# Retention feeding an erf-gated two-layer network: keys and queries of the first chunks loaded ahead of values and handled one by one, first pieces of the second layer's weights converted in single blocks

## The chip, the cores and the metric

The kernel runs on one core of a Trainium2 chip. The metric is the device time of one execution in microseconds (us). Before the change the median of seven runs is 683.71 us, with the lowest at 683.50 and the highest at 684.05 us. The core has one queue of instructions per engine, worked off in order: PE (TensorE, matrix products), DVE (VectorE, elementwise), ACT (ScalarE, copies and functions), POOL (GpSimd) and SP (SyncE, which here only issues transfers). ACT can issue transfers too, on a queue of its own. A trace of one execution shows, for every engine, when each instruction started, how long it took and what its engine had waited for.

## The reference

Two blocks follow each other. The first is a retention over 4 sequences of 768 steps, 8 heads of 64 numbers; the second is a two-layer network on the 3072 resulting rows of 512 numbers:

```python
for t in range(S):
    state = gamma[None, :, None, None] * state + np.einsum('bhd,bhe->bhde', k[:, :, t], v[:, :, t])
    y[:, :, t] = scale * np.einsum('bhd,bhde->bhe', q[:, :, t], state)
...
h = x @ w_in                                   # 512 -> 2048
sp = np.maximum(h, 0.0) + np.log1p(np.exp(-np.abs(h)))
g = h * erf(sp)
return (g @ w_out).astype(np.float32)          # 2048 -> 512
```

Keys, queries and values are 32-bit floats. The two weight matrices arrive as 64-bit floats, and the kernel turns them into 32-bit floats itself.

## The kernel before, in words

**Retention.** A sequence is cut into chunks of 128 steps, 24 chunks in all, numbered j. `load(j)` issues the transfers of a chunk's keys, queries and values, 256 KB each. `ret_scale(j)`, called `K_`, multiplies keys and queries by powers of the decay on DVE (L403, one instruction of 1024 columns for both). `ret_transpose(j)`, called `T`, transposes the keys and then the queries on PE, four instructions each (L418), and ACT copies each result out of PSUM (L424). `ret_scores(j)`, `S_`, forms the products of keys and queries on PE (L431) in two PSUM banks. `ret_mask(j)`, `M`, multiplies both banks by the causal mask on DVE (L443, two instructions of 512 columns). `ret_out(j)`, `O_`, adds on PE the part that comes from the state (L471), the part that comes from this chunk's values (L478) and the chunk's own contribution to the state (L487); ACT copies the output out (L498). `ret_add(j)`, `A`, adds the contribution to the state on DVE (L611, L613). `by` is the decay over one chunk; from it and `d_k` come the scales `kq_s` of all chunks, computed by a few small instructions on DVE and POOL (`other_scales` finishes them).

**Network.** The first four chunks make one column block of 512 rows. Its first layer has 16 pieces `hidden(g, u)` (four matrix products each, L664), four per group g; after each, ACT copies the result out (L682). `gate(g)` runs softplus (L624) and erf (L634) on ACT, each after a load of its function table; `gated(g)` multiplies on DVE (L653). `project(g, tt)` is the second layer (L700), 16 products a group into four PSUM tiles. The work on rows after the first 512 uses seven products in place of eight on sums of blocks (L757, L829) and is not touched by the change.

**Weights.** They are converted in 16 pieces in the order in, in, in, in, out, out, in, in, out, out and so on (`conversion(n)`): DVE masks the exponent (L213), ACT turns it into a scale (L214), DVE extracts and combines the mantissa (L217, L222, L225) and multiplies (L231). The first four pieces are converted in two halves of 512 columns; from the fifth on a piece is one block of 1024 columns. From the sixth on, the L213 of the following piece is slipped in ahead of L225, so that ACT's share is ready when its turn comes. `need(...)` runs the conversion up to a named block before its first use; `pace(n)` and `pace_around(n)` run further steps of it between the other work, by a running account `room`.

**What sets the order.** The program is written in the order in which each engine's queue works it off; there is no scheduler. DVE, ACT and PE each stop at the first instruction whose inputs or buffers are not there, and all behind it waits. The pool `ps_r` has two PSUM tiles in use for transposes, scores and outputs after the first four chunks: the outputs of chunk 5 go into the two tiles from which its mask L443 has read the scores. The transfers stand on SP's queue in the order k0, q0, v0, k1, v1, k2, v2, k3, q3, first half of weight piece 0, v3, other weights; q1 and q2 are issued by ACT. `keep_warm(n)` issues n products of the identity on PE whose result nobody uses (L377), each seen as two matmul records: 16 ahead of the first transposes and 3 after them.

Of the kernel before, what the change touches and what calls it, by code (L numbers as in the profile page):

```python
# [12 lines left out]
F32 = mybir.dt.float32  # L13
# [3 lines left out]
ALU = mybir.AluOpType  # L17
PSUM = bass.MemoryType.PSUM

P = 128  # L20
C = 128
TCH = 512
FG = 4
# [22 lines left out]
def kernel(  # L46
# [35 lines left out]
    ctx.enter_context(tc.manual_schedule())  # L82


    KQ, V, KB = {}, {}, {}

    NB = JPC + 2
# [12 lines left out]
    def load(j):  # L100
        b, c = divmod(j, NC)
        if j == JPC - 1:

            x = act.tile([P, N], F32, name="e", bufs=1)
            KQ[j] = x[:, : 2 * d_model].rearrange("p (i h d) -> p i h d", i=2, h=H)
            V[j] = x[:, 2 * d_model : 3 * d_model].rearrange("p (h d) -> p h d", h=H)
        else:
            KQ[j] = loads.tile([P, 2, H, D], F32, name="kq")
            V[j] = loads.tile([P, H, D], F32, name="v")
        now = slice(c * C, (c + 1) * C)  # L110
        if j >= NB:
            KB[j] = loads.tile([P, HP * C], F32, name="kb", bufs=2)
            nc.sync.dma_start(KQ[j][:, 0], k[b, :, now, :].rearrange("h p d -> p h d"))
            load_blocks(KQ[j][:, 1].rearrange("p h d -> p (h d)"), q[b, :, now, :])
            load_blocks(KB[j], k[b, :, now, :])
        for i, src in enumerate((k, q) if j < NB else ()):

            queue = nc.scalar if i and 0 < j < 3 else nc.sync
            queue.dma_start(KQ[j][:, i], src[b, :, now, :].rearrange("h p d -> p h d"))  # L119
        if j == JPC - 1:  # L120
            load_piece(0, 0)
        nc.sync.dma_start(V[j], v[b, :, now, :].rearrange("h p d -> p h d"))  # L122

    kq_s = const.tile([P, NC, 2, H], F32, name="kq_s")
    d_k = const.tile([P, H], F32, name="d_k")
# [61 lines left out]
    def conversion(n):  # L187

        which, i = pieces[n]
        half, s, at = i // 4, i % 4 // 2, i % 2

        for part in range(2) if n < 4 else (None,):
            words = raws[place[n]].bitcast(U32)
            if which == "in":
                f = slice(at * 2 * P, (at + 1) * 2 * P)
                if part is not None:
                    f = slice((at * 2 + part) * P, (at * 2 + part + 1) * P)
                to = w_in_sb[:, s, 2 * half : 2 * half + 2, :, f].rearrange("p d k f -> p (d k) f")  # L200
            else:
                to = w_out_sb[:, s, 2 * half : 2 * half + 2, at * 2 : at * 2 + 2, :].rearrange(
                    "p d f c -> p d (f c)"
                )
            words = words.rearrange("p (a b w) -> p a b w", a=to.shape[1], w=2)
            number, power = (
                x.rearrange("p (a b) -> p a b", a=to.shape[1]) for x in (numbers, powers[n % 2])
            )
            if part is not None:
                f = slice(part * P, (part + 1) * P)  # L210
                words, number, power = words[:, :, f], number[:, :, f], power[:, :, f]
            lo, hi = words[:, :, :, 0], words[:, :, :, 1]
            nc.vector.tensor_scalar(power, hi, 0x7FF00000, None, op0=ALU.bitwise_and)  # L213
            nc.scalar.activation(power, power, AF.Relu, bias=below, scale=8.0)  # L214
            if part is None:
                yield
            nc.vector.tensor_scalar(  # L217
                number, hi, 0xFFFFF, 1 << 20, op0=ALU.bitwise_and, op1=ALU.bitwise_or
            )
            yield  # L220
            numberf = number.bitcast(F32)
            nc.vector.scalar_tensor_tensor(numberf, number, 2.0**32, lo, op0=ALU.mult, op1=ALU.add)  # L222
            if part is None:
                yield
            nc.vector.scalar_tensor_tensor(  # L225
                power, hi, 1 << 31, power, op0=ALU.bitwise_and, op1=ALU.bitwise_or
            )
            if part != 0:
                load_pieces_after(n)
            yield  # L230
            nc.vector.scalar_tensor_tensor(  # L231
                to, numberf, 2.0**-52, power.bitcast(F32), op0=ALU.mult, op1=ALU.mult,
            )
            done.update((which, 2 * i + u) for u in (range(2) if part is None else (part,)))
            yield
# [18 lines left out]
    def weights():  # L254


        pending = [conversion(n) for n in range(n_p)]
        begun = 0
        for n, steps in enumerate(pending):
            for k, _ in enumerate(steps, start=begun):  # L260
                yield
                if n > 4 and n + 1 < n_p and k == 2:
                    next(pending[n + 1])
                    yield
            begun = int(n > 4)
            if pieces[n] == ("out", 5):
                yield from sums("in", 0)

# [25 lines left out]
    ident = const.tile([P, P], F32, name="ident")  # L294
    make_identity(nc, ident)
    nc.scalar.dma_start(d_k, decay_k)
    for s in range(2):
        nc.scalar.dma_start(d_s[:, s], decay_s[s * D : s * D + 1, :].to_broadcast([P, HP]))
    load(0)

    nc.scalar.copy(idle_out, ident[:, :1])
    for j in range(1, JPC):
        load(j)
    load_piece(0, 1)
    for n in range(1, 4):
        load_piece(n, 0, 1)
    load(JPC)

    causal = const.tile([P, C], F32, name="causal")
    nc.gpsimd.memset(causal, 1.0)  # L310
# [20 lines left out]


    by = const.tile([P, H], F32, name="by")
    nc.vector.reciprocal(by.rearrange("p (h s) -> p s h", s=2), d_s)
    for c in range(1, NC):
        nc.gpsimd.tensor_tensor(kq_s[:, c, 0], kq_s[:, c - 1, 0], by, op=ALU.mult)

    def other_scales():
        query_scale(slice(1, NC))

# [24 lines left out]
    QT, KT, SC, AM, XC, SU = {}, {}, {}, {}, {}, {}  # L367

    psum_turn = itertools.cycle((ps_r, ps_h))
    early = True  # L370


    idle = ps_o.tile([P, P], F32, name="o0")
# [2 lines left out]
        for _ in range(n):  # L376
            nc.tensor.matmul(idle, ident, ident, start=True, stop=True)  # L377

    keep_warm(16)

    def ret_psum(pool=None):

# [2 lines left out]

    scaled = set()

    def ret_scale(j):
        if j >= NJ:
            return  # L390
        scaled.add(j)
        if j >= NB:
            nc.vector.tensor_tensor(
                KQ[j][:, 0], KQ[j][:, 0],
                kq_s[:, j % NC, 0, :, None].to_broadcast([P, H, D]), op=ALU.mult,
            )
            for i, x in enumerate((KB[j], KQ[j][:, 1].rearrange("p h d -> p (h d)"))):
                x = x.rearrange("p (u a d) -> p u a d", u=HP, d=32)
                by = kq_b[:, j % NC, i, :, :, None].to_broadcast([P, HP, 4, 32])
                nc.vector.tensor_tensor(x, x, by, op=ALU.mult)  # L400
            return
        by = kq_s[:, j % NC, :, :, None].to_broadcast([P, 2, H, D])
        nc.vector.tensor_tensor(KQ[j], KQ[j], by, op=ALU.mult)  # L403
        pace(-1.1)

    def ret_transpose(j):
        assert j in scaled
        if j >= NB:
            for name, store, x in (
# [3 lines left out]
                nc.vector.transpose(store[j].rearrange("p u t -> p (u t)"), x)  # L413
            return
        for i, (name, store) in enumerate((("k", KT), ("q", QT))):
            p = ret_psum()
            for u in range(HP):
                nc.tensor.transpose(  # L418
                    p[:, u, :],
# [25 lines left out]
            )  # L445
        pace(-1.2)

    RP = {}

    def ret_out(j, between=None, copies=True):  # L450
        c = j % NC
        m, i = divmod(j, JPC)
        if i == 0:
            XC[m] = ret.tile([P, HP, TCH], F32, name="xT")

        if between is None:
            pp = [ret_psum() for _ in range(2)]
        else:
            pp = [ps_o.tile([P, HP, C], F32, name=f"o{r + 1}") for r in range(2)]

        def place(h):
            return pp[h % 2][h // 4 * D : (h // 4 + 1) * D, h % 4 // 2, :]
# [20 lines left out]
        if c < NC - 1:  # L483
            new = SU[j] = pp[0][:, 2:, :].rearrange("p a (b d) -> p (a b) d", d=D)
            for h in range(H):
# [2 lines left out]
                    new[r * D : (r + 1) * D, h // 2, :], KQ[j][:, 0, h, :], V[j][:, h, :],  # L488
                    start=False, stop=True, skip_group_check=True,
                )  # L490
        RP[j] = pp
        if copies:
            ret_copy(j)

    def ret_copy(j):
        m, i = divmod(j, JPC)
        for r in range(2):
            nc.scalar.copy(XC[m][:, r::2, i * C : (i + 1) * C], RP[j][r][:, :2, :])  # L498
        pace(2.5)


# [117 lines left out]
    def gate(g):  # L619
# [3 lines left out]
        E[g] = act.tile([P, N], F32, name=name, bufs=1)  # L623
        nc.scalar.activation(E[g], HS[g], AF.Softplus)  # L624

        if g:
            gate_erf(g)

    def gate_erf(g):
# [59 lines left out]
    def project(g, tt):  # L689
# [3 lines left out]
        if g:  # L693
            of = [(tt, u) for u in range(FG)]
        else:
            of = [(step % 2 * 2 + i // 2, step // 2 * 2 + i % 2) for i in range(4)]
        need("out", g * FG + max(u for _, u in of))
        for tt, u in of:
            ft = g * FG + u
# [174 lines left out]
    )  # L874


    K_(0)
    other_scales()
    T(0)
    keep_warm(3)  # L880
    for j in range(JPC - 2):
        S_(j)

        K_(j + 1)
        if j:
            A(j - 1)
        T(j + 1)
        M(j)
        O_(j)


    S_(JPC - 2)
    A(JPC - 3)
    M(JPC - 2)
    ret_out(JPC - 2, copies=False)
    K_(JPC - 1)

    next(weight_steps)
    T(JPC - 1)
    ret_copy(JPC - 2)  # L900
    need("in", 0)
    S_(JPC - 1)
    A(JPC - 2)
    M(JPC - 1)
    need("in", 1)
    early = False
    ret_out(JPC - 1, lambda: hidden_of(0, slice(TCH - C)))
    room = 0.0


# [24 lines left out]
    for g in range(G0):  # L935
# [10 lines left out]
        if g:  # L946
            for tt in range(TT):
                project(g - 1, tt)
                if g == 1 and tt < 2:
                    waiting.append((K_, 5) if tt else (M, 4))  # L950
                elif g == G0 - 1 and tt == 0:
                    waiting.extend([(K_, JPC + 2), (T, JPC + 2)])
                elif g == G0 - 1 and tt == 1:
# [132 lines left out]
```

## Time and profile before

| what | value |
|---|---|
| median of 7 runs | 683.71 us |
| the profiled execution | 684.01 us, span 682.3 us |
| PE busy | 676.3 us (99% of the span) |
| DVE busy | 389.8 us (57%); 57.35 of the 60 us from 25 to 85 us |
| ACT busy | 256.0 us (38%) |
| bytes moved | 47.65 MB, a mean of 70 GB/s; 192 to 260 GB/s in the first 68 us |

Times in the trace are counted from the start of the span. The profiled execution lies 0.30 us above the median and outside its span 1.7 us pass. Three stages matter here. Up to about 25 us PE works on the retention of the first four chunks, and inputs arrive. From 25 to about 110 us PE has work without gaps, and DVE is nearly full as well, since it converts all weights in that time. After that DVE and ACT have time to spare. "Busy" of PE is modelled, and the share over the whole span says little of the first stage, which is 4% of it.

### The profile page before, as it was taken

The page shows a single profiled execution, that of the slowest core. Times are in us where ns is not written, and L with a number is a line of the kernel's source. Part 1 is how long each engine was busy: PE and PEld are TensorE (multiplying, and loading weights), DVE is VectorE, ACT ScalarE, POOL GpSimd, SP SyncE. Part 2 cuts the span into 40 slices and gives each one's busy share as a digit, 9 for nine tenths or more (in the row PEclk, how much of TensorE's full clock was granted, in tenths as well). Part 3 has the DMA queues.
Part 4 walks back from the last instruction along what each step waited for, and adds up shares of the span by engine and source line. Part 5 has one row for each costly group of instructions (what it writes and reads, how often), then busy time and mean ns, then how long its engine had stood idle before and what let it go on. Part 6 is the DMA issues. An engine that isn't in the chain of part 4 may idle for free.

```text
span 682.3 us, 14444 instructions
## 1 busy us (share of the span) xinstructions
PE 676.3 (99%) x6214; PEld 578.6 (85%) x6214; DVE 389.8 (57%) x609; ACT 256.0 (38%) x291; POOL 5.8 (1%) x21
## 2 busy tenths in 40 slices
PE   9999999999999999999999999999999999999998
PEld 8744544587999999999999999999999999999996
DVE  4899999585945634643553564555544554343224
ACT  3368362424424234144144242341441441423431
POOL 2000000100000000000000000000000000000000
PEclk9999999999999999999999999999999999999999
DMA  9999644333412322222321222222312200000000
GB/s 192 227 260 238 164 125 103 62 61 63 114 35 45 76 37 42 75 41 37 78 45 32 63 46 45 68 42 44 72 35 49 58 18 2 1 32 1 1 32 32
DMA packets 156528, 47.65 MB, mean 70 GB/s; under 512 B 143024, under 2 KB 147376, under 8 KB 156464
## 3 DMA queue, kind: packets, MB, share of 16 engines
q1 hardware_dynamic: 153952, 46.19, 31.2%
q8 instruction: 49, 0.80, 0.5%
q10 hardware_dynamic: 2512, 0.53, 0.5%
q14 instruction: 15, 0.12, 0.1%
HBM read 40.39 MB, written 6.29 MB: 68 GB/s over the span
## 4 chain that ended last, share of the span: by engine, by line
PE 96%; SPq 2%; DMA 1%; DVE 0%; ACT 0%; issue 0%; DVEq 0%
PE hp L757 37%; PE o L829 36%; PE hp L664 8%; PE o L700 8%; PE r L543 1%; PE hp L508 1%; SPq L119 1%; PE o L579 1%; DMA w_out_sb<-in_moe_w_in_dram 1%; PE r L431 1%; PE hp L558 1%; SPq L122 1%; PE r L558 1%; PE r L478 0%; PE r L418 0%; PE r L579 0%
## 5 line engine op out<-in xcount | busy, mean ns | idle before, releaser
L757 PE MATMUL hp<-xs,w_in_sb 128*128 128x128 f32 x1280 | 149.7, 275 | 0.0
L757 PEld LDWEIGHTS hp<-xs,w_in_sb 128*128 128x128 f32 x1280 | 147.8, 192 | 1.6 <-issue 0.5
L829 PE MATMUL o<-w_out_sb,h 128*128 128x256 f32 x640 | 141.7, 379 | 0.0
L829 PEld LDWEIGHTS o<-w_out_sb,h 128*128 128x128 f32 x640 | 121.6, 190 | 16.5
L757 PE MATMUL hp<-xT,w_in_sb 128*128 128x128 f32 x960 | 113.7, 275 | 0.0
L757 PEld LDWEIGHTS hp<-xT,w_in_sb 128*128 128x128 f32 x960 | 111.9, 192 | 1.9 <-issue 1.0
L829 PE MATMUL o<-w_out_sb,e 128*128 128x256 f32 x480 | 112.1, 383 | 0.0
L653 DVE TENSOR_TENSOR e<-h,e 128x1024 f32<-128x1024 f32 x42 | 49.5, 1221 | 100.0 <-ACT e L634 100.0
L829 PEld LDWEIGHTS o<-w_out_sb,e 128*128 128x128 f32 x480 | 88.2, 190 | 11.6
L664 PE MATMUL hp<-xT,w_in_sb 128*128 128x512 f32 (+2 forms) x144 | 56.8, 548 | 0.0
L782 DVE TENSOR_TENSOR h<-h,hp 128x512 f32<-128x512 f32 x20 | 13.8, 688 | 72.3 <-PE hp L757 72.3
L624 ACT ACT_TABLE_LOAD x24 | 30.8, 1283 | 60.8 <-issue 45.4
L664 PEld LDWEIGHTS hp<-xT,w_in_sb 128*128 128x128 f32 x144 | 25.7, 190 | 26.7 <-issue 24.3
L634 ACT ACTIVATE e<-e 128x2048 f32<-128x2048 f32 (+1 forms) x23 | 42.1, 1836 | 0.2
L624 ACT ACTIVATE e<-h 128x2048 f32<-128x2048 f32 x22 | 42.0, 1910 | 0.2
L770 DVE TENSOR_TENSOR h<-h,hp 128x512 f32<-128x512 f32 x20 | 13.8, 688 | 41.9 <-PE hp L757 41.9
L775 ACT COPY h<-hp 128x512 f32<-128x512 f32 x20 | 11.7, 586 | 61.0 <-PE hp L757 61.0
L780 ACT COPY h<-hp 128x512 f32<-128x512 f32 x20 | 11.7, 585 | 60.3 <-PE hp L757 60.3
L773 ACT COPY h<-hp 128x512 f32<-128x512 f32 x20 | 11.7, 585 | 57.1 <-PE hp L757 57.1
L597 ACT COPY xT<-r 128x256 f32<-128x256 f32 x32 | 10.4, 375 | 54.8 <-PE r L543 54.8
L634 ACT ACT_TABLE_LOAD x24 | 30.8, 1283 | 0.4
L768 ACT COPY h<-hp 128x512 f32<-128x512 f32 x20 | 11.8, 588 | 48.6 <-PE hp L757 48.6
(136 smaller groups left out, 673.9 us busy)
## 6 DMA issues: line engine op xcount, KB each, us to landing
w_out_sb<-in_moe_w_out_dram SPq DMA_DIRECT2D x14, 512.0 KB, 5.7
kq<-in_k_dram SPq DMA_DIRECT2D x23, 256.0 KB, 3.9
v<-in_v_dram SPq DMA_DIRECT2D x23, 256.0 KB, 3.1
out_dram<-r SPq DMA_DIRECT2D x23, 256.0 KB, 3.1
kq<-in_q_dram SPq DMA_DIRECT2D x288, 16.0 KB, 1.8
kb<-in_k_dram SPq DMA_DIRECT2D x288, 16.0 KB, 1.7
w_in_sb<-in_moe_w_in_dram SPq DMA_DIRECT2D x8, 512.0 KB, 6.9
w_out_sb<-in_moe_w_in_dram SPq DMA_DIRECT2D x8, 256.0 KB, 7.4
```

The costliest lines, as they stand in the source:

```text
L558: nc.tensor.matmul(other[a][own, u % 2, D:] if crossed else pp[a][own, u % 2, t], V[j][t, 2 * u + r, :], AM[j][t, r, u, :D], start=crossed ...
L624: nc.scalar.activation(E[g], HS[g], AF.Softplus)
L634: nc.scalar.activation(E[g][:, half], E[g][:, half], AF.Erf)
L653: nc.vector.tensor_tensor(E[g][:, half], HS[g][:, half], E[g][:, half], op=ALU.mult)
L664: nc.tensor.matmul(HP_[ft][:, t], w_in_of(ft, kk), XC[0][:, kk, t], start=(kk == 0), stop=(kk == n_k - 1),)
L700: nc.tensor.matmul(O[0][tt].rearrange("p (d c) -> p d c", d=2), E[g][:, u * TCH + tt * P : u * TCH + (tt + 1) * P], w_out_of(ft), start=(f ...
L757: nc.tensor.matmul(bank[:, u, :], w_in_sb[:, s, IN[a], kk, u * P : (u + 1) * P], XS[m][b][:, kk, :], start=(p in (1, 2, 5) and u == 0 and ...
L768: nc.scalar.copy(h["11"], flat)
L770: nc.vector.tensor_tensor(h["11"], h["11"], flat, op=ALU.add)
L773: nc.scalar.copy(h["12"], flat)
L782: nc.vector.tensor_tensor(h["12"], h["12"], flat, op=ALU.add)
L829: nc.tensor.matmul(O[m][i][:, half, :], G[g][a][:, u * P : (u + 1) * P], w_out_sb[:, s, OUT[b], u, :], start=i not in started, stop=(s == ...
```

## The change

- Transfers of chunks 0 to 3: all on SP, in the order k0, q0, k1, q1, v0, k2, q2, v1, k3, q3, v2, first half of weight piece 0, v3. `d_s` is one transfer of both halves.
- Keys and queries of these chunks are scaled by two instructions of 512 columns and transposed separately; the scores, masks, outputs and state additions stand between them in a new order. The scales of chunk 1 are computed right after the first keys are scaled (`second_scales`). The outputs of chunks 0 to 3 go into the four tiles of `ps_o`.
- Identity products: 7, 2, 1 and 2 at four places.
- `A(2)` stands before the conversion of the first half of weight piece 0 (`need("in", 0)`).
- The fifth and sixth piece of weights (the first two of the second layer) are converted in two halves each, without the early L213 of the next. `project(0, tt)` takes block tt for all four row tiles, in place of two blocks for two tiles.
- erf of group 1 is issued after `project(0, 0)`, behind one more conversion step, and `M(4)`, `K_(5)` after `project(0, 2)`, behind the conversion of the seventh piece.

```diff
         for i, src in enumerate((k, q) if j < NB else ()):
-            queue = nc.scalar if i and 0 < j < 3 else nc.sync
-            queue.dma_start(KQ[j][:, i], src[b, :, now, :].rearrange("h p d -> p h d"))
-        if j == JPC - 1:
-            load_piece(0, 0)
-        nc.sync.dma_start(V[j], v[b, :, now, :].rearrange("h p d -> p h d"))
+            nc.sync.dma_start(KQ[j][:, i], src[b, :, now, :].rearrange("h p d -> p h d"))
+        if not early:
+            load_values(j)
...
-        for part in range(2) if n < 4 else (None,):
+        for part in range(2) if n < 6 else (None,):
...
-                if n > 4 and n + 1 < n_p and k == 2:
+                if n > 5 and n + 1 < n_p and k == 2:
                     next(pending[n + 1])
                     yield
-            begun = int(n > 4)
+            begun = int(n > 5)
...
-    for s in range(2):
-        nc.scalar.dma_start(d_s[:, s], decay_s[s * D : s * D + 1, :].to_broadcast([P, HP]))
+    nc.scalar.dma_start(d_s, decay_s[::D].rearrange("(o s) h -> o s h", o=1).to_broadcast([P, 2, HP]))
     load(0)
     nc.scalar.copy(idle_out, ident[:, :1])
     for j in range(1, JPC):
         load(j)
+        load_values(j - 1)
+    load_piece(0, 0)
+    load_values(JPC - 1)
     load_piece(0, 1)
...
+    def second_scales():
+        nc.vector.reciprocal(by.rearrange("p (h s) -> p s h", s=2), d_s)
+        nc.vector.tensor_tensor(kq_s[:, 1, 0], kq_s[:, 0, 0], by, op=ALU.mult)
+        query_scale(1)
+        for c in range(2, NC):
+            nc.gpsimd.tensor_tensor(kq_s[:, c, 0], kq_s[:, c - 1, 0], by, op=ALU.mult)
...
-    keep_warm(16)
+    keep_warm(7)
...
-        by = kq_s[:, j % NC, :, :, None].to_broadcast([P, 2, H, D])
-        nc.vector.tensor_tensor(KQ[j], KQ[j], by, op=ALU.mult)
+        part = slice(i, i + 1) if i is not None else slice(2)
+        x = KQ[j][:, part]
+        by = kq_s[:, j % NC, part, :, None].to_broadcast([P, x.shape[1], H, D])
+        nc.vector.tensor_tensor(x, x, by, op=ALU.mult)
...
-        if g:
+        if g > 1:
             gate_erf(g)
...
-            of = [(step % 2 * 2 + i // 2, step // 2 * 2 + i % 2) for i in range(4)]
+            of = [(i, step) for i in range(TT)]
...
-    K_(0)
-    other_scales()
-    T(0)
-    keep_warm(3)
-    for j in range(JPC - 2):
-        S_(j)
-        K_(j + 1)
-        if j:
-            A(j - 1)
-        T(j + 1)
-        M(j)
-        O_(j)
-    S_(JPC - 2)
-    A(JPC - 3)
-    M(JPC - 2)
-    ret_out(JPC - 2, copies=False)
-    K_(JPC - 1)
-    next(weight_steps)
-    T(JPC - 1)
-    ret_copy(JPC - 2)
-    need("in", 0)
-    S_(JPC - 1)
-    A(JPC - 2)
-    M(JPC - 1)
+    K_(0, 0)
+    second_scales()
+    T(0, 0)
+    keep_warm(2)
+    K_(0, 1)
+    T(0, 1)
+    keep_warm(1)
+    K_(1, 0)
+    T(1, 0)
+    S_(0)
+    K_(1, 1)
+    T(1, 1)
+    keep_warm(2)
+    other_scales()
+    M(0)
+    S_(1)
+    K_(2, 0)
+    T(2, 0)
+    O_(0)
+    M(1)
+    K_(2, 1)
+    T(2, 1)
+    A(0)
+    O_(1)
+    K_(3, 0)
+    T(3, 0)
+    S_(2)
+    A(1)
+    M(2)
+    O_(2)
+    K_(3, 1)
+    T(3, 1)
+    A(2)
+    need("in", 0)
+    S_(3)
+    M(3)
     need("in", 1)
...
-                if g == 1 and tt < 2:
-                    waiting.append((K_, 5) if tt else (M, 4))
+                if g == 1 and tt == 0:
+                    need("out", 1)
+                    next(weight_steps)
+                    gate_erf(1)
+                elif g == 1 and tt == 2:
+                    need("in", 2 * FG + 1)
+                    waiting.extend([(M, 4), (K_, 5)])
```

## The prediction

> **What bounds the kernel now.** I read the page's chain of work first, then busy time by stretch, then the timelines of the first 95 us, since the change touches nothing later. The chain's shares by engine and two stretches (us, busy time of PE, PEld, DVE, ACT, POOL, clock, DMA share, GB/s):
>
> ```profile
> PE 96%; SPq 2%; DMA 1%; DVE 0%; ACT 0%; issue 0%; DVEq 0%
> ...
> 25.00:45.00 20.00, 20.00 (x109) 11.50 (x106) 18.20 (x34) 9.04 (x14) 0.00 (x0) 1.00 1.13 256
> 45.00:65.00 20.00, 20.00 (x67) 9.55 (x66) 19.39 (x23) 16.09 (x17) 0.00 (x0) 1.00 1.07 247
> 65.00:85.00 20.00, 20.00 (x103) 10.06 (x103) 19.76 (x23) 8.32 (x11) 0.00 (x0) 1.00 0.66 167
> ```
>
> PE has no gap from 25 us on, so a change ahead of that counts only if PE also stays fed. DVE has 2.65 idle us in these 60. The timeline of DVE (start, duration, line, idle before):
>
> ```profile
> 11.04 0.69 DVE L443 TENSOR_TENSOR am<-r,causal 128x512 f32<-128x512 f32 x1 [0.47 <-PE hp L431]
> ...
> 19.46 0.69 DVE L443 TENSOR_TENSOR am<-r,causal 128x512 f32<-128x512 f32 x1 [0.25 <-PE hp L431]
> 20.07 0.68 DVE L443 TENSOR_TENSOR am<-hp,causal 128x512 f32<-128x512 f32 x1
> 20.67 1.22 DVE L403 TENSOR_TENSOR e<-e,kq_s 128x1024 f32<-128x1024 f32 x1
> 21.80 0.42 DVE L213 TENSOR_SCALAR w_out_sb<-w_out_sb 128x512 uint32<-128x512 uint32 x1
> ...
> 24.53 0.41 DVE L611 TENSOR_TENSOR state<-state,r 128x256 f32<-128x256 f32 x1
> 25.18 0.69 DVE L443 TENSOR_TENSOR am<-r,causal 128x512 f32<-128x512 f32 x1 [0.24 <-PE hp L431]
> ...
> 86.83 1.23 DVE L222 SCALAR_TENSOR_TENSOR w_out_sb<-w_out_sb,w_in_sb 128x1024 f32<-128x1024 uint32 x1
> 87.98 1.28 DVE L443 TENSOR_TENSOR am<-r,causal 128x512 f32<-128x512 f32 x2
> ```
>
> The weight conversion starts at 21.80, and behind it stands everything up to M(5) at 87.98. The timeline of PE at both ends, and L471's own waits:
>
> ```profile
> 1.46 6.79 PE L377 MATMUL o<-ident 128*128 128x128 f32 x32 [1.46 <-POOL ident masks.py:199]
> 8.09 0.60 PE L418 MATMUL r<-ident,kq 128*128 128x128 f32 x4
> ...
> 89.24 0.73 PE L471 MATMUL r<-qT,state 64*64 64x128 f32 x16
> 89.91 1.09 PE L478 MATMUL r<-am,v 128*64 128x128 f32 x16
> ...
>   DVE am L443: 0.8, 1
> ```
>
> O(5) may overwrite its two PSUM tiles only when M(5) has read them, the second at 87.98+1.28 = 89.26. PE arrives at 89.24. So at this place DVE and PE finish together: PE gains nothing here unless M(5) comes earlier, and any delay of M(5) reaches the end. ACT in the stretch where the change alters the conversion:
>
> ```profile
> 48.40 0.59 ACT L682 COPY h<-hp 128x512 f32<-128x512 f32 x1 [1.15 <-PE hp L664]
> 49.34 1.15 ACT L214 ACTIVATE w_out_sb<-w_out_sb,below 128x1024 uint32<-128x1024 uint32 x1 [0.35 <-DVE w_out_sb L213]
> 50.51 1.28 ACT L634 ACT_TABLE_LOAD   x1
> 51.80 1.91 ACT L634 ACTIVATE e<-e 128x2048 f32<-128x2048 f32 x1
> 53.62 0.57 ACT L682 COPY h<-hp 128x512 f32<-128x512 f32 x1
> ```
>
> Now ACT forms the fifth piece's scale once, ahead of erf's table load.
>
> **Part 1, transfers and early chunks: where the conversion starts.** I work at the clock of the profiled execution, where a filler pass takes 6.79/32 = 0.21 us and a transpose after 8 us 0.11.
>
> Transfers. Landing is issue plus the listed time: k0 0.81+3.2 = 4.0, q0 1.31+4.4 = 5.7, v0 1.94+4.9 = 6.8, k1 2.92+5.8 = 8.7, q1 4.05+5.2 = 9.3, v1 4.39+6.0 = 10.4. On one queue I give places instead: k1 third at 6.8, q1 fourth at some 8.1, v0 fifth at 9.3, k2 sixth at 10.4 (before 5.38+7.5 = 12.9, for which DVE waited 0.54). SP issues q1 and q2 too (0.4 to 1.4 us each), but it runs 5 us ahead of the landings. The values come up to 3 us later and are used after 12.7; covered. The weights keep their places (13.78+6.2 = 20.0).
>
> Chain. K(0,0) 512 wide 0.69, ends 4.7; its transposes 4 x 0.21 and two fillers end 6.5. The two d_s transfers landed at 4.2 and 5.5, which bounds the single one; I take 5.2. Four small instructions at 0.22, then K(0,1) to 6.75; its transposes end 7.7. Behind a filler, T(1,0) and ACT's copy (0.58), S(0) runs from 8.7 and takes 1.09, so M(0) is at 9.85 against 11.04. K(1,1) and the other scales end 9.35, POOL's four products before that: covered. M(0) and K(2,0) fill DVE to 11.75; S(1) holds PE to 12.2 and T(2,0) to 12.7; O(0) takes 0.82+0.67, ACT's copy 0.38 (A waits for it in the trace), A(0) 0.42: 15.1. O(1) 0.6+0.82+0.67, T(3,0) 0.5 and S(2) 1.09 lead to M(2) at 18.9 against 19.46.
>
> So the chunks gain 0.55. But the conversion had begun 2.34 after M(2) (a second mask and K(3)). Now A(2) stands ahead of it: O(2) ends 2.6 after M(2) (19.46 to 22.08), copy 0.4, A(2) 0.34, with handovers 3.5. It starts at 22.4, **0.6 later**, though its data is there at 20.0. Seven fillers fewer save nothing further, since PE waits at these places.
>
> **Part 2, DVE from the conversion's start to M(5), 66.18 us before.**
> - Out: A(2) 0.33, the wait ahead of M(3) 0.24, 0.3 of two waits of L225 for ACT (0.76, 0.44), 0.16 ahead of `gated(0)`: -1.0.
> - Two pieces in halves: four blocks of 2.74 (26.39 to 29.11 and the like) for two of 4.97 (48.62 to 53.59): +1.0.
> - In the changed order one L222 of 1024 columns stands behind M(5): -1.15.
> - New wait 1. The second half's scale stands on ACT behind erf(0) and a copy. From the first half's L213: ACT starts at 0.45, then 0.63 + 1.29 + 1.82 + 0.47 + 0.72 (the pitches of the rows above, halves from the 512-wide L214) = 5.4. DVE reaches its L225 at 4.15 (2.74 and three steps). It waits **1.25**, and `gated(0)` behind it.
> - New wait 2. The sixth piece's second scale stands behind softplus(1): 0.45 + 0.63 + 1.29 + 1.82 + 0.72 = 4.9 against 4.15: **0.78**.
>
> Moved: M(4) now stands behind the seventh piece. From K(5) to M(5) are 19.7 us (68.28 to 87.98); M(4)'s 1.2 join that stretch, and L222, L213 and L225 (1.14, 0.60, 1.25) and the L222 of 1.15 leave it, so M(4) comes 16.8 before M(5), at 72.6. O(4) takes its tiles at 74.1 by PE's gain of 0.4: covered by 0.2 (second mask 73.9); if M(5) came later, M(4) would too, and PE would lose the same time there first, not twice. erf(1) moves from 64.90 to some 66, used by `gated(1)` after M(4): covered.
>
> Together +0.85. Bounds of the two waits: 0, if ACT gets ahead, and 3.2 each (a table load and a function, 1.28+1.91), if ACT reaches them late; the sums of rows lie between and I keep them.
>
> **Sum.** M(5) moves to 87.98+0.6+0.85 = 89.4, PE's second L471 from 89.31 to 90.75. PE itself would be ready at 88.8: the first layer starts behind the first conversion (22.4+2.8 = 25.2) at 25.25 against 25.68. The other needs are met (`project(0,1)` needs out 1 near 57, PE is there at 60). PE stands still for 1.9 us, and what follows is unchanged: 684.01 + 1.4 = 685.4 for an execution like the profiled one, which lies 0.3 above the median: **685.1 us**.
>
> **A rule beside a row.** The row: 28 filler passes of 0.21 us pass without a gap from 1.46 to 7.6 before the pace doubles. With 7 fillers there are gaps, of 0.15 us near 4.7 and of 0.3 near 6.6. If they don't matter, the above stands. If 6.1 us without a gap are needed, counted from 6.8, the clock opens at 12.9: 5.3 us at half pace cost 2.65, of which waits cover some 0.6, so +2.0 and 687.1.
>
> The Trainium skill, "TensorE: Matmul & The Clock Gate", Part 1, says that the clock opens after a free-running window of 3413 ns has been busy, whatever the number of matmuls; seven fillers last 3.0 us. If a gap spoils a window, its estimate is an opening between 10.2 and 13.6, and 686 to 687.4.
>
> **Rivals.**
> - Late clock, 687.1, as worked out. For it: no gapless 6 us before 6.8. Against: the gaps are a tenth of the time.
> - ACT's waits are hidden (the copies and functions come earlier than DVE): 2.03 goes, M(5) is at 87.4, and PE arrives by its own gain of 0.4: 683.6, less 0.3, **683.3**. Against: both queues are in order, and erf needs all of `h`.
> - The other side, faster: the chunks end so early that the conversion starts as its data lands, at 20.0. That is 1.8 earlier; with +0.85, M(5) gains 1.0: 682.7. It decides when the first L213 starts before 20.95. Against: M(2) would have to start at 16.5.
> - No effect: the waits gone (2.03) and gains lost alike, 683.7.
>
> **How the numbers follow.** About 0.2% (1.4 us: 682.3 and 685.1) is what a measurement can tell. Forecast 0.45, half of it above 685.1; late clock 0.28; ACT's waits hidden 0.15; the early conversion 0.07; no effect 0.05. Slower 0.22+0.28 and a little for larger waits, 0.55; same 0.40; faster 0.05, from the early conversion with ACT's waits hidden as well. Range from 683.3 to 687.2; the forecast's own is 684.4 to 685.8.
>
> **What would show it.** First L213 near 22.4, behind A(2); two idle times of DVE ahead of L230 (the old L225) ended by ACT, 1.25 and 0.78; the fifth M near 89.4 and PE idle some 1.9 ahead of the state part of O(5). The pace of transposes near 8 us (0.11 or 0.21) tells of the clock. I am wrong if the first conversion starts before 21, or if DVE doesn't wait for ACT between 50 and 63 us.

## The result and the profile after

The changed kernel takes 685.34 us (median of 15 runs; 14 of them between 685.14 and 685.61, one at 687.17), against 683.64 us for the kernel before (35 runs). The ratio is 1.0026, with a 95% interval of 1.002 to 1.0033. The change made the kernel 1.7 us slower; the prediction was 685.1 us, 0.24 below the measured median. Its profiled execution took 685.3 us with a span of 683.6.

In the changed kernel the lines have moved: the mask is L460, the state addition L620, the conversion L218 to L236 (ACT's part L219, the instruction that needs it L230), the first layer L673, the state part of an output L486, the second layer L709.

The chain of work of the changed kernel, shares of the span by engine. Before, DVE had 0% of it; now it passes through DVE:

```profile
PE 89%; DVE 6%; ACT 2%; issue 2%; DMA 1%; SPq 0%; ACTq 0%; DVEq 0%
```

Busy time by stretch (us, PE, PEld, DVE, ACT, POOL, clock, DMA share, GB/s). PE was busy all the time from 25 us on (the last stretch of before stands first here, the others stand with the prediction); now it stands still in three of the four stretches:

```profile
85.00:95.00 10.00, 10.00 (x64) 5.19 (x61) 9.83 (x12) 6.86 (x9) 0.00 (x0) 1.00 0.52 171
...
25.00:45.00 20.00, 19.82 (x90) 11.26 (x91) 18.67 (x35) 9.56 (x14) 0.00 (x0) 1.00 1.06 226
45.00:65.00 20.00, 20.00 (x67) 9.65 (x66) 17.35 (x31) 14.19 (x17) 0.00 (x0) 1.00 1.04 244
65.00:85.00 20.00, 19.48 (x97) 9.54 (x97) 19.76 (x22) 9.78 (x13) 0.00 (x0) 1.00 0.71 175
85.00:95.00 10.00, 9.34 (x63) 4.93 (x62) 9.86 (x12) 4.81 (x7) 0.00 (x0) 1.00 0.52 179
```

The first of the three is the wait for the first converted weights at 25 us. DVE lost 2 us between 45 and 65 us (19.39 busy before, 17.35 now). The timeline of DVE tells where (start, duration, line, idle time before and what ended it):

```profile
18.75 0.69 DVE L460 TENSOR_TENSOR am<-r,causal 128x512 f32<-128x512 f32 x1 [0.84 <-PE hp L448]
...
21.89 0.42 DVE L620 TENSOR_TENSOR state<-state,o 128x256 f32<-128x256 f32 x1 [1.25 <-ACT xT L507]
22.23 0.42 DVE L218 TENSOR_SCALAR w_out_sb<-w_out_sb 128x512 uint32<-128x512 uint32 x1
...
53.63 0.69 DVE L230 SCALAR_TENSOR_TENSOR w_out_sb<-w_out_sb 128x512 uint32<-128x512 uint32 x1 [1.31 <-ACT w_out_sb L219]
...
62.15 0.69 DVE L230 SCALAR_TENSOR_TENSOR w_in_sb<-w_out_sb,w_in_sb 128x512 uint32<-128x512 uint32 x1 [0.83 <-ACT w_in_sb L219]
...
80.29 0.41 DVE L620 TENSOR_TENSOR state<-state,r 128x256 f32<-128x256 f32 x1
...
89.33 1.28 DVE L460 TENSOR_TENSOR am<-r,causal 128x512 f32<-128x512 f32 x2
```

The two waits for ACT stand in the second halves of the fifth and the sixth weight piece, as predicted, and M(5), the mask of chunk 5, starts at 89.33. What ACT did ahead of the first of these waits, on its own timeline: the first half's scale, then erf's table load, erf, a copy, and only then the second half's scale, although its input had been there since 51.3.

```profile
48.56 0.72 ACT L219 ACTIVATE w_out_sb<-w_out_sb,below 128x512 uint32<-128x512 uint32 x1
49.30 1.28 ACT L643 ACT_TABLE_LOAD   x1
50.59 1.92 ACT L643 ACTIVATE e<-e 128x2048 f32<-128x2048 f32 x1
52.41 0.56 ACT L691 COPY h<-hp 128x512 f32<-128x512 f32 x1
52.88 0.72 ACT L219 ACTIVATE w_out_sb<-w_out_sb,below 128x512 uint32<-128x512 uint32 x1
```

And what PE then waited for, on its timeline. It stops ahead of the second half of T(5), because A(4) on DVE has not yet read the PSUM tile that these transposes overwrite, and again ahead of O(5), because M(5) has not read its two. The 32 products of the second layer behind O(5) start at 92.28; before (the last line) they started at 90.93:

```profile
25.18 2.82 PE L673 MATMUL hp<-xT,w_in_sb 128*128 128x384 f32 x8 [0.67 <-DVE w_in_sb L236]
...
80.76 0.66 PE L435 MATMUL r<-ident,kq 128*128 128x128 f32 x4 [0.52 <-DVE state L620]
...
90.07 0.43 PE L486 MATMUL r<-qT,state 64*64 64x128 f32 x2 [0.50 <-DVE am L460]
90.67 0.66 PE L486 MATMUL r<-qT,state 64*64 64x128 f32 x14 [0.17 <-DVE am L460]
...
92.28 14.00 PE L709 MATMUL o<-w_out_sb,r 128*128 128x512 f32 x32
...
90.93 14.00 PE L700 MATMUL o<-w_out_sb,r 128*128 128x512 f32 x32
```

The spans of the two profiled executions differ by 1.3 us, the start of these products by 1.35: the whole difference has arisen by then.

### The profile page after: what moved, and what is told of

Same layout as the page of the kernel before. It is cut to its first block, busy times and chain, and to the rows that moved or that the text cites. A ratio compares the mean times of both kernels' runs of the same rounds, so it can differ in the third digit from the quotient of the medians.

```text
span 683.6 us, 14431 instructions
## 1 busy us (share of the span) xinstructions
PE 674.6 (99%) x6200; PEld 575.7 (84%) x6200; DVE 391.4 (57%) x626; ACT 256.9 (38%) x293; POOL 5.9 (1%) x20
## 4 chain that ended last, share of the span: by engine, by line
PE 89%; DVE 6%; ACT 2%; issue 2%; DMA 1%; SPq 0%; ACTq 0%; DVEq 0%
PE hp L766 37%; PE o L838 36%; PE o L709 6%; PE hp L673 3%; PE r L552 1%; PE hp L517 1%; PE o L588 1%; DMA kq<-in_k_dram 1%; DVE w_out_sb L230 1%; DVE w_in_sb L230 1%; DVE w_out_sb L222 1%; PE r L448 1%; PE hp L567 1%; PE o L493 1%; PE r L567 1%
## 5 line engine op out<-in xcount | busy, mean ns | idle before, releaser
L673 PE MATMUL hp<-xT,w_in_sb 128*128 128x512 f32 (+2 forms) x144 | 56.8, 548 | 0.7 <-DVE w_in_sb L236 0.7
L633 ACT ACT_TABLE_LOAD x24 | 30.8, 1283 | 60.8 <-issue 45.4
L673 PEld LDWEIGHTS hp<-xT,w_in_sb 128*128 128x128 f32 x144 | 25.7, 190 | 27.4 <-issue 24.8
L784 ACT COPY h<-hp 128x512 f32<-128x512 f32 x20 | 11.7, 586 | 61.0 <-PE hp L766 61.0
L789 ACT COPY h<-hp 128x512 f32<-128x512 f32 x20 | 11.7, 585 | 60.3 <-PE hp L766 60.3
L782 ACT COPY h<-hp 128x512 f32<-128x512 f32 x20 | 11.7, 585 | 57.1 <-PE hp L766 57.1
L643 ACT ACT_TABLE_LOAD x24 | 30.8, 1283 | 0.4
```

Of the source, the lines that this page charges most:

```text
L643: nc.scalar.activation(E[g][:, half], E[g][:, half], AF.Erf)
L673: nc.tensor.matmul(HP_[ft][:, t], w_in_of(ft, kk), XC[0][:, kk, t], start=(kk == 0), stop=(kk == n_k - 1),)
```

## The experiments

The start of the second layer's products behind O(5), "the mark" from here on, is read in every trace; the part of the span behind it was 591.3 or 591.4 us in all of them. The theory (D) was that time is lost only by way of DVE's queue: what stands ahead of M(5) in that queue, and when it starts. The rivals were that the clock opens later (C), that the new transfers cost or bring something by themselves (T), and that the halves and their waits cost time wherever the masks stand (W).

### Each part alone

The changed kernel with the conversion, erf of group 1, `project(0, tt)`, `M(4)` and `K_(5)` as before:

```diff
-        for part in range(2) if n < 6 else (None,):
+        for part in range(2) if n < 4 else (None,):
...
-        if g > 1:
+        if g:
             gate_erf(g)
...
-                if g == 1 and tt == 0:
-                    need("out", 1)
-                    next(weight_steps)
-                    gate_erf(1)
-                elif g == 1 and tt == 2:
-                    need("in", 2 * FG + 1)
-                    waiting.extend([(M, 4), (K_, 5)])
+                if g == 1 and tt < 2:
+                    waiting.append((K_, 5) if tt else (M, 4))
```

> The changed kernel with the old conversion of the fifth and sixth weight piece (whole blocks), the old place of erf(1), the old order of project(0, tt) and the old places of M(4) and K(5): the chunk part of the change alone. Theory D (DVE's queue up to M(5) sets the end; what made it longer are two waits for ACT of 1.31 and 0.83): the first conversion starts at 22.2 as in the changed kernel, both waits are gone, M(5) stands near 87.5, and PE is held up by less than 0.3 us at O(5): 683.2, 0.4 below the kernel before. Theory C (the later opening of the clock or the gaps in the first 10 us cost the time): 685.3, since that stage is unchanged. Theory T (values and weights that land later, weights at 21.4 in place of 19.9): 685.3 as well.

Measured: 683.55 us (683.31 to 683.79, 11 runs) against 683.69 before, ratio 0.9997 (0.9988 to 1.0005). Theory D had put it at 683.2; a gain over the kernel before is not shown.

The kernel before with only that part (the same lines, the other way round):

> The kernel before with only the conversion part of the change: halves for the fifth and sixth piece, erf(1) behind project(0, 0), project(0, tt) by block, M(4) and K(5) behind project(0, 2). Theory D: the start of the conversion is 21.8 as before, the two waits of DVE for ACT appear (1.3 and 0.8), M(5) moves by +1.0 for the halves, -1.15 for the L222 behind it and +2.1 for the waits, to 89.9: 685.5, 1.9 above the kernel before, so slower than the whole change. Theories C and T: 683.6, since the chunks are the old ones.

Measured: 685.54 us (685.36 to 685.94, 8 runs), ratio 1.0026 (1.0016 to 1.0037).

So the early part is worth -0.14 us (not to be told from nothing), the conversion part +1.85, and both together +1.70: within the intervals they add, and the new transfers, the new early order and its fewer identity products have no share in the slowdown. DVE's stretch from the first conversion to M(5) shows the same division. It was 66.18 us before; it is 65.26 with the early part alone (22.07 to 87.33), 68.05 with the conversion part alone (21.45 to 89.50, the lines below), and 67.10 with both:

```profile
21.45 0.42 DVE L216 TENSOR_SCALAR w_out_sb<-w_out_sb 128x512 uint32<-128x512 uint32 x1
...
89.50 1.28 DVE L446 TENSOR_TENSOR am<-r,causal 128x512 f32<-128x512 f32 x2
```

The same trace corrects a reading of the one before. Its early part is that of the kernel before, and its first conversion begins at 21.45, not at 21.80: the profiled execution of before was late by 0.35 from the start, and it lay 0.3 above its median. The clock tells why: by the traces' record of the granted clock it opened to full speed at 7.67 us there and at 5.71 here, the 32 passes of the identity products took 6.79 us against 5.85, and the first transposes came at 8.09 against 7.26.

### The scale formed whole

The changed kernel, where for the fifth and sixth piece the exponent mask and ACT's scale of both halves are formed in one instruction each ahead of the first half; all else stays in halves:

```diff
+            words_all, power_all = words, power
...
-            nc.vector.tensor_scalar(power, hi, 0x7FF00000, None, op0=ALU.bitwise_and)
-            nc.scalar.activation(power, power, AF.Relu, bias=below, scale=8.0)
+            if n < 4 or part != 1:
+                if n in (4, 5):
+                    all_hi, all_power = words_all[:, :, :, 1], power_all
+                else:
+                    all_hi, all_power = hi, power
+                nc.vector.tensor_scalar(all_power, all_hi, 0x7FF00000, None, op0=ALU.bitwise_and)
+                nc.scalar.activation(all_power, all_power, AF.Relu, bias=below, scale=8.0)
```

> The changed kernel, in which the exponents of the fifth and sixth piece are masked and turned into scales for the whole piece at once, ahead of the first half; the rest stays in halves. ACT's share is then done ahead of erf(0) and softplus(1). Theory D: the two waits (2.1 together) go, some 0.2 a piece comes back because the first half's L230 waits for a scale of 1024 columns; M(5) near 87.6, PE no longer held up for more than 0.3 at O(5): 683.2 to 683.6. If only the number of conversion instructions counted, nothing would change: 685.3.

Measured: 683.72 us (683.49 to 685.46, 11 runs), ratio 1.0001 (0.9992 to 1.001). The timeline of DVE in this kernel (its L236 is the changed kernel's L230): each piece now waits 0.15 us for ACT, and M(5) is 1.72 earlier.

```profile
49.99 0.69 DVE L236 SCALAR_TENSOR_TENSOR w_out_sb<-w_out_sb 128x512 uint32<-128x512 uint32 x1 [0.15 <-ACT w_out_sb L225]
...
58.00 0.69 DVE L236 SCALAR_TENSOR_TENSOR w_in_sb<-w_out_sb,w_in_sb 128x512 uint32<-128x512 uint32 x1 [0.15 <-ACT w_in_sb L225]
...
87.61 1.28 DVE L466 TENSOR_TENSOR am<-r,causal 128x512 f32<-128x512 f32 x2
```

The same for one piece alone (`n == 4`, then `n == 5`, in place of `n in (4, 5)`):

> The changed kernel with the scale of the fifth weight piece alone formed whole ahead of its halves; the sixth as in the changed kernel. Theory D: the wait of 1.31 us goes down to some 0.15, the one of 0.83 stays, M(5) near 88.2, and PE has its second tile 0.5 us later than with both whole: 684.3 us. Rival W2 (the waits hide each other: without the first, the second grows by as much, or one of them costs nothing): 685.3 us or 683.7 us.

> The changed kernel with the scale of the sixth weight piece alone formed whole ahead of its halves; the fifth as in the changed kernel. Theory D: the wait of 0.83 us goes down to some 0.15, the one of 1.31 stays, M(5) near 88.6: 684.8 us. Rival W2 (the waits hide each other, or one of them costs nothing): 685.3 us or 683.7 us.

Measured: 684.31 us (684.14 to 684.62) with the fifth whole, 684.50 us (684.32 to 684.89) with the sixth, 11 runs each; against 683.81 for before in this comparison the ratios are 1.0008 (1.0000 to 1.0017) and 1.0012 (1.0003 to 1.002). Each of the two waits costs time of its own, and neither hides the other. By the medians the fifth's, 1.31 long, brings 1.03 when it goes, the sixth's, 0.83 long, brings 0.84, and both together 1.62; the difference from the sum, 1.87, is smaller than the intervals allow to tell (0.0009 of the time is 0.6 us). The traces say that they add: DVE's stretch from the first conversion to M(5) is 0.98 shorter with the fifth whole (22.51 to 88.63), 0.71 with the sixth (22.37 to 88.76) and 1.72 with both (22.23 to 87.61).

### The waits left, the masks moved

The changed kernel with both waits, but the mask and state addition of chunk 4 and the mask of chunk 5 each two conversion steps earlier in DVE's queue (K(5) and `gated(1)`, which stand between them, come earlier with them):

```diff
-            ([(S_, 5), (M, 5)], []),
+            ([(S_, 5), (M, 5), (pace, 2)], []),
...
+            if (g, u) == (1, 3):
+                room -= 2
```

> The changed kernel with the masks of chunks 4 and 5 and the state addition of chunk 4 each two conversion steps (some 1.8 us) earlier on DVE; both new waits for ACT stay. Theory D (the waits cost time only by way of DVE's queue to the fifth chunk's mask): M(5) near 87.5 instead of 89.33, no stall of PE ahead of O(5) and of T(5), second-layer products L709 near 90.6 instead of 92.28, 683.7 us. Rival W (the waits, or the halves themselves, cost their time wherever the masks stand, by later weights or later activations): 685.3 us. Rival C (the clock): 685.3 us.

Measured: 683.48 us (683.26 to 685.48, 11 runs), ratio 1.0000 (0.9991 to 1.0008). The timeline of DVE still has both waits, and M(5) at the place where PE needs it:

```profile
53.61 0.69 DVE L230 SCALAR_TENSOR_TENSOR w_out_sb<-w_out_sb 128x512 uint32<-128x512 uint32 x1 [1.30 <-ACT w_out_sb L219]
...
62.13 0.69 DVE L230 SCALAR_TENSOR_TENSOR w_in_sb<-w_out_sb,w_in_sb 128x512 uint32<-128x512 uint32 x1 [0.82 <-ACT w_in_sb L219]
...
87.46 1.30 DVE L460 TENSOR_TENSOR am<-r,causal 128x512 f32<-128x512 f32 x2
```

The timeline of PE has no gap ahead of O(5), and the mark is at 90.44 in place of 92.28:

```profile
88.69 0.79 PE L486 MATMUL r<-qT,state 64*64 64x128 f32 x16
89.41 1.09 PE L493 MATMUL r<-am,v 128*64 128x128 f32 x16
```

This is the experiment that decides between D and W. The halves, their waits for ACT and the later conversions are all there, and the 1.86 us are gone. The waits cost time because small instructions on which PE depends stood behind them; beyond that nothing is left that can be measured.

Which of them? M(4) was covered: in the changed kernel PE starts O(4) at 73.96 without a gap. That leaves A(4) and M(5). The mask of chunk 5 alone moved, and then the two of chunk 4 alone:

```diff
-            ([(O_, 4), (A, 4)], []),
+            ([(O_, 4), (A, 4), (pace, -2)], []),
...
-            ([(S_, 5), (M, 5)], []),
+            ([(S_, 5), (M, 5), (pace, 2)], []),
```

> The changed kernel with the mask of chunk 5 alone two conversion steps (some 1.8 us) earlier on DVE; the mask of chunk 4 and the state addition of chunk 4 where they were. In the changed kernel PE stands still in two places, ahead of T(5) for the state addition (0.52 us) and ahead of O(5) for the mask (0.67 us). If the first stall is time of its own (theory S): the second goes, the first stays, L709 near 91.1, 684.0 us. If the first stall is covered by something behind it (theory H): 683.5 us, as with all three moved.

```diff
-            ([(O_, 4), (A, 4)], []),
+            ([(O_, 4), (A, 4), (pace, 2)], []),
...
+            if (g, u) == (1, 3):
+                room -= 2
```

> The changed kernel with the mask of chunk 4 and the state addition of chunk 4 two conversion steps earlier on DVE; the mask of chunk 5 where it was, near 89.3. PE no longer stands still ahead of T(5), comes 0.5 us earlier to O(5) and waits there as much longer: 685.3 us, unchanged (theories S and H alike). If instead the stall ahead of T(5) sets the end by itself: 684.8 us.

Measured: 684.18 us (683.96 to 684.45, 11 runs; ratio 1.0008, 0.9999 to 1.0017) and 685.51 us (685.42 to 687.13, 5 runs; ratio 1.0037, 1.0025 to 1.005). The timeline of PE with the two of chunk 4 moved: no stop at T(5), and in return 1.42 us ahead of O(5), where there were 0.50.

```profile
90.15 0.43 PE L486 MATMUL r<-qT,state 64*64 64x128 f32 x2 [1.42 <-DVE am L460]
90.75 0.66 PE L486 MATMUL r<-qT,state 64*64 64x128 f32 x14 [0.17 <-DVE am L460]
```

The later stop covers the earlier one completely, but not the other way round. With M(5) moved alone the stop at T(5) remains and costs 0.70 us by the medians, 0.67 by the mark (91.11 against 90.44).

### An earlier conversion

The changed kernel with A(2) behind the conversion of the first half piece, in place of ahead of it:

```diff
     T(3, 1)
-    A(2)
 
     need("in", 0)
+    A(2)
     S_(3)
     M(3)
```

> The changed kernel with A(2) behind the conversion of the first half of weight piece 0 instead of ahead of it. Theory D: the conversion starts when its data lands (21.4) in place of 22.2, so M(5) and the end come 0.8 earlier less A(2)'s 0.33: 684.8. If PE's stop at O(5) had another cause than DVE's queue: 685.3.

Measured: 686.00 us (685.89 to 687.73, 5 runs), ratio 1.0036 (1.0024 to 1.0049): a miss with the wrong sign. The conversion did start 1.2 us earlier, as the timeline of DVE shows, but ACT was at the copies of O(2) and of the queries until 22.6, so that the first L230 waited, and A(2) came 2.8 later than in the changed kernel:

```profile
21.04 0.43 DVE L218 TENSOR_SCALAR w_out_sb<-w_out_sb 128x512 uint32<-128x512 uint32 x1 [0.39 <-DMA w_out_sb<-in_moe_w_in_dram]
...
23.37 0.69 DVE L230 SCALAR_TENSOR_TENSOR w_out_sb<-w_out_sb 128x512 uint32<-128x512 uint32 x1 [0.83 <-ACT w_out_sb L219]
...
24.70 0.41 DVE L620 TENSOR_TENSOR state<-state,o 128x256 f32<-128x256 f32 x1
...
31.45 0.69 DVE L230 SCALAR_TENSOR_TENSOR w_in_sb<-w_out_sb,w_in_sb 128x512 uint32<-128x512 uint32 x1 [1.01 <-ACT w_in_sb L219]
```

PE needs A(2) for O(3), which stands in its queue ahead of the first layer. The timeline of PE: it waited there, and the first layer began at 25.77 in place of 25.18.

```profile
25.17 0.67 PE L486 MATMUL o<-qT,state 64*64 64x128 f32 x16 [1.24 <-DVE state L620]
25.77 2.85 PE L673 MATMUL hp<-xT,w_in_sb 128*128 128x384 f32 x8
```

That delay of 0.6 put off the following copies on ACT, the wait at 31.45 grew from 0.47 to 1.01, M(5) came at 89.97, and the mark is 0.64 later. The expectation had followed DVE and forgotten who waits for A(2).

A version that takes this into account: both scales whole, the masks earlier, ACT's first scale ahead of the copies of O(2), A(2) behind the first half, and the first products of the first layer ahead of O(3). Only the edits that were not shown above stand here:

```diff
     M(2)
-    O_(2)
     K_(3, 1)
+    next(weight_steps)
+    O_(2)
     T(3, 1)
-    A(2)
 
     need("in", 0)
     S_(3)
+    hidden_of(0, slice(TCH - C))
+    A(2)
     M(3)
     need("in", 1)
-    ret_out(JPC - 1, lambda: hidden_of(0, slice(TCH - C)))
+    ret_out(JPC - 1)
```

> Both scales whole, masks of chunks 4 and 5 and state addition two steps earlier, and at the start: the first exponent mask and scale ahead of the copies of O(2) on ACT, A(2) behind the first conversion half, the first layer's first products ahead of O(3). Theory D: first conversion on DVE near 21.0 instead of 22.2 with no wait for ACT behind it, first products of the first layer on PE near 24.5 instead of 25.2, PE without a gap from there: 683.1 us. If what PE does ahead of 25 us is bound by something else (rival T, transfers): 683.6 us.

Measured: 683.47 us (682.86 to 685.16, 11 runs), ratio 0.9996 (0.9987 to 1.0005). The profiled execution, at 683.74 one of the slower ones, shows on DVE's timeline why it is no better: the first conversion waits for its weights.

```profile
21.57 0.43 DVE L224 TENSOR_SCALAR w_out_sb<-w_out_sb 128x512 uint32<-128x512 uint32 x1 [0.71 <-DMA w_out_sb<-in_moe_w_in_dram]
```

ACT's scale now stands ahead of the copy of the last queries, so that PE, too, waits for the weights, 1.59 us ahead of S(3). The first layer starts at 24.92 in place of 25.18 in the changed kernel, but O(3) follows it and PE is back at the first layer at 29.79, against 29.42. None of the versions here is faster than the kernel before beyond what can be measured; four are faster than the changed one by 1.6 to 1.9 us.

### The clock

The changed kernel with one identity product in place of twelve:

```diff
-    keep_warm(7)
+    keep_warm(1)
...
-    keep_warm(2)
     K_(0, 1)
     T(0, 1)
-    keep_warm(1)
     K_(1, 0)
...
-    keep_warm(2)
     other_scales()
```

> The changed kernel with one identity product in place of the twelve (7, 2, 1 and 2). Rival C (the pace of PE doubles only after PE has been busy for some us; the fillers bring that ahead of the first chunks): the pace doubles later than 8 us, the early chunks are late by what waits do not cover, 687.1 us or more in every run, like the single run of the changed kernel at 687.17. Theory D without a clock: the fillers hide nothing, 685.3 us.

Measured: 686.84 us (686.31 to 689.07, 4 runs), ratio 1.0054 (1.0034 to 1.0074). The timeline of PE: four transposes take 1.12 us up to 11 us and 0.66 at 13.5; in the changed kernel (the last two lines) they take 0.66 from 6.52 on.

```profile
7.54 1.11 PE L435 MATMUL r<-ident,kq 128*128 128x128 f32 x4
...
10.59 1.12 PE L435 MATMUL hp<-ident,kq 128*128 128x128 f32 x4
...
13.48 0.66 PE L435 MATMUL r<-ident,kq 128*128 128x128 f32 x4
...
1.46 3.36 PE L389 MATMUL o<-ident 128*128 128x128 f32 x14 [1.46 <-POOL ident masks.py:199]
...
6.52 0.66 PE L435 MATMUL hp<-ident,kq 128*128 128x128 f32 x4 [0.52 <-DVE kq L418]
```

The first conversion starts at 23.89, 1.66 later than in the changed kernel, and the mark is at 93.96, 1.68 later. The median rose by 1.50. That is the clock's part, as rival C had it, though 687.1 or more did not come in every run: three of the four lie between 686.31 and 686.99.

## Why the prediction was right, by its steps

**What bounds the kernel.** Right. DVE and PE met at O(5), any delay of M(5) reached the end, and the experiments with the masks and A(4) moved show that beside them nothing did that can be measured.

**Part 1, the early chunks.** M(0) was predicted at 9.85 and came at 9.49, M(2) at 18.9 and came at 18.75, the first conversion at 22.4 and came at 22.23, behind A(2), which waits for ACT's copy. The single d_s transfer landed at 4.34 (taken: 5.2), so that the scales of chunk 1 were never waited for. The second transfer of the first weights landed at 21.40, not 20.0; with A(2) ahead of the conversion this was covered, and in the version with A(2) behind and the scale ahead it became the bound.

**Part 2, DVE's stretch.** Predicted +0.85, measured +0.92 (67.10 against 66.18). The two waits were put at 1.25 and 0.78 and measured 1.31 and 0.83; the rows of before for table load, function, copy and scale gave both within 0.06. The terms that part 1 takes out of the stretch (A(2), the wait ahead of M(3), 0.3 of two waits for ACT: 0.87) measured 0.92 with the early part alone, and the rest of the sum (+1.72) measured +1.87 with the conversion part alone.

**M(5), PE, the end.** M(5) at 89.4 (measured 89.33), PE's second L486 at 90.75 (90.67), PE standing still for 1.9 us. Against the version with the masks moved, which starts the first layer at the same time, the mark is 1.84 later: right as a sum, but not at one place. (The idle times on PE's rows, 0.52, 0.50 and 0.17, add to less, since the ends of matmuls are modelled.) The step that said PE would lose time "there first, not twice" looked at M(4) and O(4), which was covered indeed, and left out A(4), which frees the PSUM tile for T(5): part of the 1.84 is lost at T(5) already. For the total it made no difference, as the two moves alone show, and that was luck: the stop that was counted happens to be the later one and covers the other. Whoever had moved only M(5) would have kept 0.70 us of the loss.

**The last term of the sum.** The 685.4 for an execution like the profiled one came out at 685.3. But the prediction then took 0.3 off, the distance of the profiled execution of before to its median. The changed kernel's profiled execution lies at its median, and what was 0.3 late in the old one was the start of the conversion (21.80, against 21.45 in the trace with the same early part), behind a clock that had opened late; the new early part does not inherit that. Taking that one trace, which lies at the median of its kernel, as the typical one, the early part moved the start by 0.78, not by 0.43, and 0.78 with the 0.92 of part 2 make the 1.70 between the medians. This term is the mis-sized one, by 0.24 us: 685.34 in place of 685.1.

**The rivals.** "ACT's waits are hidden" and "no effect" fell with the two idle times on DVE. "The early conversion" needed a start before 20.95; the weights alone would have allowed that in most of the eleven traces with the new transfers (their second transfer landed between 19.3 and 21.5 us, at 21.4 in the changed kernel's). A(2), which stands ahead and waits until ACT has copied O(2) out, forbade it: it starts at 21.89. The late clock is not seen in the profiled execution: transposes ran at the full pace from 6.5 us on in spite of the gaps around the fillers, so the reading that 6.1 us without a gap are needed was wrong; 14 of 15 runs lie within 0.5 us of it. Its price, 2.0 us for an opening at 12.9, was somewhat high: with one filler and an opening at 12.2 it was 1.50. The run at 687.17 is where this rival was put, but its trace was not taken, and that the clock was its cause is not shown.

**The rule beside the row.** The trace's record of the granted clock begins with the opening to full speed: at 5.1 us in the changed kernel, where PE was busy from 1.46 us to 4.8 and nearly so to 5.4; with one filler at 12.2, after transposes and scores had kept PE busy from 7.5 to 11.7 us with hardly a gap. In the ten traces with all twelve identity products and the new early part it lies between 4.3 us (M(5) moved alone) and 7.7 (both scales whole). There the four transposes at 6.55 still took 1.06, and yet M(0) stood at 9.49 and M(2) at 18.76, as in the changed kernel: an opening that late cost nothing that can be seen. The Trainium skill, "TensorE: Matmul & The Clock Gate", Part 1, says that the clock opens after one busy free-running window of 3413 ns. These traces agree with it only if a window need not be busy from end to end: the opening at 4.3 us comes 2.8 us after PE's first product at 1.46. The pace there bears the record out: the transposes at 4.79 took 0.66.

## What to carry to other kernels

When a conversion is cut into halves whose middle step runs on another engine, ask what that engine's queue holds between the halves: here a table load and a function, 3.2 us, stood between two scales of 0.72. A wait on an engine that is not the bound costs nothing by itself; look for the small instructions behind it that free a buffer of the bounding engine, and move those ahead of the waiting work, all of them, since the stop that comes first is hidden by the later one and appears only when that one is gone. Before taking a difference of two profiled executions over to the medians, see how far each lies from its own.

## What the runs showed of the hardware that was not expected

**Single executions are later with the new early part.** Of the 106 runs of the eleven kernels that have the new transfers and the shorter identity products (the changed kernel and all experiments but the conversion part alone), eight lay 1.5 to 2.3 us above their median; of the 114 runs of before that stood beside them, and of the 8 with the conversion part alone, none lay more than 0.8 above. The size fits a clock that opens much later (1.50 us with one filler), and fewer identity products leave less margin for that, but no such run was profiled. The runs' mean granted clock settles it in part: it is 0.997 or 0.998 in three of the eight, and 0.999 or 1.000 in every other run of any kernel here, so in these three the clock was lower for longer. The other five have 1.000, but so has the profiled execution with one filler, whose clock opened at 12.2 us: the record begins only with the opening. The cause of the eight stays open.

**A table load needs no further pause here.** The Trainium skill, "ScalarE: Activation LUTs", section "What ACT_TABLE_LOAD costs", gives 1283 ns and a drain of some 1380 ns for a switch. The trace has the load at 1.28 us, starting 0.02 us after the scale ahead of it had ended, and erf 1.29 us behind the load's start: no drain on either side. With it the two waits would have been longer by that much; the rows gave them within 0.06.
